# One attention-plus-MLP kernel: loads from three issuing queues instead of one, with a new order of its stages

## The chip, the cores and the metric

The kernel runs on one core of one Trainium2 chip. The metric is the device time of one launch in microseconds: 155.31 us, the median of three runs (155.22 to 155.47).

## What is computed

The inputs are r, k, v, w of shape 4 x 8 x 768 x 48 (batch, heads, sequence, head dimension), u (8 x 48), and the weights of an MLP (384 to 1024 to 384, with a gain vector of 1024), all float32. Two parts follow one another, a recurrence over time and an MLP:

```
for t in range(S):
    cur = einsum("bhd,bhe->bhde", u[None] * k[t], v[t])
    y[t] = einsum("bhd,bhde->bhe", r[t], state + cur)
    state = w[t][..., None] * state + einsum("bhd,bhe->bhde", k[t], v[t])
x = y, laid out as 3072 tokens x 384
h = x @ w_in
solu = h * softmax(h)
out = layernorm(solu) * g_ln @ w_out          # 3072 x 384
```

## The kernel before

The work is cut into 24 units, each of 128 time steps of one batch (six chunks of the sequence times four batches, chunk by chunk). A unit goes through two parts.

Attention: its w, k, r and v are loaded (LW, LK, LR, LV, lines 246 to 256; each 128 partitions x 8 heads x 48 floats, so 1024 pieces of 192 bytes). ScalarE takes the logarithm of w (lw), TensorE cumulates it over time (cum), ScalarE makes the decays of it in PSUM (ex), VectorE multiplies k and r with them (kp), TensorE transposes both (krk, krr) and ScalarE or VectorE copies the result out (kr). TensorE makes the scores (M), which are masked and copied (m; on VectorE with the mask, on ScalarE with a later sel on GpSimd). GpSimd makes the bonus term of u (p, q, in part qh, and dv; VectorE adds up dg). TensorE makes the output of the chunk (Y), which is copied (y), and the new state (S, then et and st).

MLP: x is transposed (X, copied by xT), TensorE makes the hidden layer (H, line 469: 24 matmuls that need all three parts of w_in), ScalarE its exponential (e), VectorE the product (he), ScalarE, VectorE or GpSimd its square (hq), GpSimd in some units the sum of the halves of e (ea), TensorE the output with the column sums for the norm (Oa, Ob, line 496), and small instructions the scale (sq, qm, lv), before ScalarE or VectorE writes the result (o) and it is stored (out, line 536).

The weights come once: w_in in three parts (LI, cast to bfloat16 by wi), w_out in two halves (LO, scaled by gw and centred by ce, with the column mean mn).

The order of everything stands in one string, ORDER (lines 21 to 67). A word is a stage's short name and its unit, and after the point the engine (a ScalarE, d VectorE, p GpSimd) or the PSUM bank. The loop in line 550 emits the stages word by word, and `InOrder` (line 72) makes each engine keep that order: an instruction never overtakes another of the same engine, and a DMA never another of the same queue. All loads and stores are issued by SyncE (SP); an issue waits until its buffer is free. There are seven input buffers of each kind (NIO, line 69), so unit 7 takes the buffers of unit 0. `hot` words are matmuls on zeros in otherwise idle TensorE time.

Of the kernel before, what the change touches and what calls it, by code (L numbers as in the profile page):

```python
# [8 lines left out]
F32 = mybir.dt.float32  # L9
BF16 = mybir.dt.bfloat16  # L10
# [11 lines left out]
LW2 LU0 ik0 lw2 hot5.4 cum2.0 LW1 lw1 us0.7 ih0 LW3 lw3 cum3.2 LR2 uc0 ex2 LK2 p2 LV2 vb2.p kp2 hot4.4 krk2.6 krr2  # L22
LR1 LK1 cum1.4 LW0 ex1 kp1 kr2.d hot1.0 S2.7 lw0 et2 LV1 vb1.d LW4 st2 p1 q1 hot2.0 krk1.1 krr1 q2 qh2 dg2 LG0
kr1.a M2.4 ex3 hot1.0 M1.6 m1.d dv2 LR0 LK0 p0 q0 cum0.0 ex0 lw4 cum4.6 ex4 kp0 krk0.1 krr0 LR3 gs0.0 gc0 dg1
m2.d Y2.i0 kr0.d LK3 p3 LR4 LV0 vb0.a dg0 dv1 kp3 Y1.i5 hot3.1 krk3.4 krr3 LK4 kp4 M0.2 m0.d krk4.1 y1.a X1.5
krr4 y2.a X2.0 dv0 xT2.d hot1.6 Y0.n7 y0.d kr3.a M3.2 hot1.0 X0.6 S1.4 p4 q3 kr4.a xT1.a xT0.a LI2 LI1 wi1.a
M4.0 m4.a et1 LI0 S0.5 et0 wi0.d m3.d LO1 wi2.p H1.6 e1 gw5.a H2.0 e2 H0.2 LO0 gw2.a q4 qh4 dg4 qh3 dg3 gw4.p
gw7.p LV3 vb3.p dv3 sel4 LW6 e0 gw6.d st1 LV4 vb4.p he1 lw6 dv4 gw1.d LW5 gw0.d gw3.d mn0.4 mc0 ce5.p ce6.p
Y3.i7 ce4.p he2 st0 he0 cum6.0 y3.a ce7.p hot1.5 X3.6 lw5 xT3.a ce3.d LK6 LR6 p6 Y4.n5 LR5 LK5 ce2.d hq0.a ex6
LW7 cum5.2 H3.6 p5 y4.d ex5 ce1.d ce0.d Oa0.5 kp6 krk6.1 krr6 S4.0 hq1.d Oa1.4 kp5 krk5.3 krr5 X4.2 Ob1 e3 he3  # L30
LV5 q6 q5 kr5.d hq2.a et4 st4 M5.6 kr6.a M6.0 xT4.d lw7 cum7.2 hq3.a sq1 m6.a m5.d dg5 vb5.d qm1 dv5 Ob0 ex7 sq0
qm0 S3.7 qh6 LR7 LK7 p7 kp7 et3 lv1 st3 lv0 H4.0 Y5.n6 y5.d LR9 LK8 o1.d e4 krk7.3 krr7 Oa2.2 he4 X5.7 q7 kr7.d
LW9 lw9 o0.a LK9 p9 LW8 lw8 S5.6 et5 cum9.4 ex9 Ob2 sq2 LR8 p8 st5 dg6 kp9 qm2 LV6 xT5.a LV9 vb6.p dv6 sel6
cum8.0 ex8 kp8 hq4.a LV7 LV11 out1 LW10 dg7 vb7.p dv7 Oa3.3 vb9.a lv2 H5.6 e5 M7.4 m7.d he5 q8 krk9.1 LK10 krr9
kr9.a S9.0 et9 Ob3 sq3 st9 q9 qm3 o2.a out0 ea5.p Y6.i5 y6.a LV8 LR10 Y7.n4 y7.d LW11 LW12 krk8.1 M9.6 lw10 lv3
X6.2 xT6.a m9.d o3.a krr8 LV10 out3 out2 kr8.d qh9 dg9 dg8 hq5.d cum10.4 ex10 kp10 S6.0 vb11.d et6 X7.2 xT7.a
st6 p10 vb8.d dv8 dv9 H6.6 e6 he6 H7.2 lw11 e7 he7 M8.4 m8.a Oa5.1 Y9.n0 Ob5 sq5 y9.d cum11.6 ex11 krk10.5 krr10
qm5 kr10.d S7.4 et7 st7 Oa4.3 hq6.d lv5 lw12 o5.a X9.2 sel8 Y8.i0 vb10.p y8.a LK11 LR11 kp11 xT9.d q10 dg10 p11
M10.4 m10.a sel10 S10.1 et10 st10 dv10 S8.0 et8 S11.7 et11 X8.6 xT8.a LK12 LW13 cum12.4 q11 ex12 lw13 st11 st8
Ob4 sq4 qm4 LW14 LR12 kp12 p12 lw14 lv4 o4.a out5 LK13 LV12 LR13 Y10.n2 dg11 y10.d H8.6 e8 krk12.1 krk11.0 krr11  # L40
krr12 kr12.d he8 kr11.a q12 qh12 cum13.4 H9.2 vb12.p S12.1 ex13 p13 q13 ea7.p dg12 kp13 dv11 LW16 LR14 LK14 e9
he9 et12 st12 M12.6 m12.a Oa6.0 X10.5 xT10.a krk13.4 krr13 kr13.a M11.6 m11.d ea8.p dv12 sel12 p14 cum14.2 ex14
q14 out4 Ob6 sq6 hq8.d M13.4 m13.d LV13 hq7.a LW15 lw15 lw16 kp14 vb13.d H10.6 dg13 qm6 LW18 lw18 Y11.n1 y11.d
Oa8.5 LK16 LR15 LR16 LK15 e10 he10 hq9.a krk14.4 Y12.i3 krr14 lv6 qh14 kr14.d p15 ea10.p dv13 LR18 LV14 vb14.p
q15 qh15 LK18 p18 Ob8 sq8 qm8 y12.a S13.2 et13 st13 o6.a lv8 X11.1 xT11.d cum16.6 ex16 X12.3 hq10.d LW19 kp16
Oa9.4 cum15.0 xT12.a Ob9 ex15 kp15 sq9 o8.a dg14 dv14 qm9 M14.2 m14.a sel14 krk16.7 Oa7.6 krr16 kr16.d lv9 o9.d
cum18.0 ex18 kp18 Ob7 LV15 S14.5 et14 st14 krk15.3 krr15 kr15.d LK19 Y13.i2 lw19 cum19.0 krk18.7 p16 q16 vb15.a
S15.4 y13.a sq7 qm7 dg15 X13.5 xT13.d ex19 LR19 kp19 lv7 o7.a q18 krr18 kr18.d H11.2 et15 st15 krk19.5 krr19
kr19.d LW17 lw17 cum17.0 e11 he11 ex17 ea11.p out8 LK17 LR17 p17 kp17 H12.6 e12 he12 hq11.a p19 H13.4 e13 Oa10.3
Y14.n2 M16.0 m16.a dg16 q19 dv15 y14.d ea12.p ea13.p M15.6 m15.d he13 Ob10 sq10 X14.2 out9 Oa11.1 LW20 qm10 lw20  # L50
cum20.6 hq12.d krk17.0 krr17 out6 out7 LV16 vb16.a dv16 xT14.a S16.2 LR20 ex20 LK20 dg18 et16 st16 lv10 o10.a
H14.4 e14 kp20 Ob11 sq11 kr17.d LK23 qm11 lv11 o11.a Oa12.2 krk20.3 krr20 kr20.a he14 sel16 Y16.n7 y16.d Y15.n6
y15.d M19.4 m19.a M18.0 m18.d Ob12 X15.7 xT15.a q17 hq13.d LV19 LW21 LV17 X16.3 xT16.a ea14.p vb19.a M17.4 m17.d
sq12 LK22 out10 qm12 dg17 qh19 vb17.p sel19 p20 hq14.a LW22 LV20 q20 qh20 dv17 M20.0 LV21 m20.d out11 LK21 H15.6
e15 he15 lw22 ea15.p H16.4 LV18 vb18.p dv18 LR21 p21 lw21 Oa14.3 Y17.n1 LR22 LV23 q21 dg19 dv19 Ob14 LR23 p23
p22 e16 he16 lv12 Oa13.0 LW23 o12.a out12 sq14 qm14 hq15.d vb20.a lv14 dg20 dv20 y17.d cum21.6 ex21 Ob13 cum22.4
sq13 ex22 LV22 vb22.p ea16.p o14.d out14 Y18.n2 y18.d Oa15.1 X18.3 qm13 kp22 lv13 xT18.d X17.2 xT17.a kp21 Ob15
sq15 qm15 S18.5 et18 st18 Y19.n4 y19.d lv15 o15.a out15 o13.a krk22.2 S17.3 et17 lw23 H18.6 e18 ea18.p hq16.d
vb21.d st17 Y20.n5 y20.d X19.4 xT19.d krr22 kr22.a H17.0 he18 hq18.d cum23.4 ex23 kp23 Oa16.3 e17 ea17.p he17
krk21.2 krr21 kr21.a H19.6 e19 krk23.5 X20.4 krr23 q22 qh21 vb23.p out13 xT20.a kr23.a he19 Oa18.2 Ob16 sq16  # L60
M21.0 q23 ea19.p qh23 dg22 dv22 m21.a sel21 qm16 lv16 M22.6 hq19.a M23.4 Ob18 sq18 dg21 H20.0 o16.a out16 m22.d
m23.d Oa19.7 Y22.n6 qm18 lv18 hq17.d Ob19 S19.5 dg23 dv23 e20 Oa17.4 y22.d X22.3 he20 et19 st19 xT22.d dv21
Y21.n6 Ob17 y21.d sq19 o18.a sq17 qm17 lv17 Y23.n1 out18 qm19 lv19 X21.0 xT21.d H22.2 o17.a e22 out17 ea20.p
y23.d H21.0 X23.5 xT23.a e21 hq20.d o19.d out19 Oa20.6 he22 hq22.d H23.4 e23 he21 hq21.d Ob20 sq20 qm20 lv20
o20.a out20 ea22.p Oa22.7 ea21.p Oa21.3 he23 hq23.d Ob22 sq22 qm22 lv22 Ob21 sq21 qm21 lv21 o21.d o22.a out22
out21 ea23.p Oa23.2 Ob23 sq23 qm23 lv23 o23.a out23
"""

NIO, NLW, NKP, NWK = 7, 10, 6, 4
# [24 lines left out]
def kernel(  # L94
# [26 lines left out]

    nc.scalar.preload_act_table_set("natural_log_exp_and_others")
# [32 lines left out]
    g_rows = consts.tile([KF, 128], F32)  # L155

# [57 lines left out]
    qm_t = ring("qm", NWK, [C, 1], F32)  # L214
    lv_t = ring("lv", NWK, [C, 1], F32)
# [30 lines left out]
    def load_w(i, x):  # L246
        sp.dma_start(out=w_t[i % NIO][:, :, :D], in_=rows_of(w, i))

    def load_k(i, x):
        sp.dma_start(out=kr_t[i % NIO][:, 0, :, :D], in_=rows_of(k, i))  # L250

    def load_r(i, x):
        sp.dma_start(out=kr_t[i % NIO][:, 1, :, :D], in_=rows_of(r, i))

    def load_v(i, x):
        sp.dma_start(out=v_t[i % NIO][:, :, :D], in_=rows_of(v, i))

    def load_u(i, x):
        sp.dma_start(out=u_row, in_=u.rearrange("(o h) d -> o (h d)", o=1))

    def load_g(i, x):
        sp.dma_start(out=g_rows, in_=moe_g_ln.rearrange("(ko ki) -> ko ki", ki=128))

    def load_w_in(j, x):
        sp.dma_start(out=win_f[:, j, :], in_=moe_w_in[j * 128:(j + 1) * 128, :])

    def load_w_out(j, x):
        part = slice(j * KF // 2, (j + 1) * KF // 2)
        sp.dma_start(out=wout_f[:, part, :],
                     in_=moe_w_out.rearrange("(ko ki) d -> ki ko d", ki=128)[:, part, :])  # L270
# [109 lines left out]

    def scores(i, x):
        kr = kr_s[i % NKP]
        m_ps = live[i]["m_ps"] = bank([C, 2, HP, C], F32, x, "m_ps")
        for hp in range(HP):
            for a in range(2):
                rows = slice(64 * a, 64 * a + 64)
                pe.matmul(m_ps[:, a, hp, :], lhsT=kr[rows, hp, :], rhs=kr[rows, HP + hp, :], start=True, stop=True)
# [80 lines left out]

    def hidden(i, x):
        xT = xT_t[i % NWK]  # L470
        h_ps = live[i]["h_ps"] = bank([128, KF, C], F32, x, "h_ps")
# [4 lines left out]

    def hidden_exp(i, x):
        act.activation(out=e_t[i % NWK], in_=live[i]["h_ps"], func=EXP)
# [7 lines left out]
    def hidden_mul(i, x):  # L486
        dve.tensor_mul(out=he_t[i % NWK], in0=live[i]["h_ps"], in1=e_t[i % NWK])

    def hidden_square(i, x):
        he, hq = he_t[i % NWK], hq_t[i % NWK]  # L490
        if x == "a":
            act.activation(out=hq, in_=he, func=SQUARE)
        else:
            (dve if x == "d" else pool).tensor_mul(out=hq, in0=he, in1=he)

    def output(i, part):
        L = live[i]
        e, he, hq, o_ps = e_t[i % NWK], he_t[i % NWK], hq_t[i % NWK], L["o_ps"]
        for f in range(part * KF // 2, (part + 1) * KF // 2):
# [84 lines left out]
```

## Time and profile before

| What | us |
|---|---|
| median of three runs | 155.31 |
| span of the profiled execution, first to last instruction | 152.4 |
| what lies around the span, against the median | 2.9 |
| busy time PE, DVE, ACT, POOL | 136.4, 131.8, 120.0, 119.0 |
| busy time of the warm-up matmuls (tile warm) | 7.8 |
| bytes moved | 27.06 MB |

The profiled execution has no launch time of its own on record, so its span stands for it and the 2.9 us are what the runs have on top. PE is TensorE's matmuls, PEld its weight loads, DVE VectorE, ACT ScalarE, POOL GpSimd, SP SyncE; SPq is SP's queue. Busy time is the union of an engine's instructions, which is a little less than the sum of their durations, since the ends of neighbours overlap. Nearly all instructions carry the line of the helper (L86), so they are told apart by the names of what they read and write.

### The profile page before, as it was taken

What the parts mean: (1) busy time and instruction counts of PE and PEld (TensorE: products, weight loads), DVE (VectorE), ACT (ScalarE), POOL (GpSimd) and SP (SyncE); (2) the same over time, 40 slices, a digit from 0 to 9 for tenths busy, and PEclk for the clock granted to TensorE, in tenths of its full rate; (3) what the DMA queues carried; (4) which work ended last, traced back from release to release, by engine and by line L of the source; (5) the groups of instructions that cost most, each with busy time, mean ns of one, the idle gap of its engine ahead of it and who ended that gap; (6) DMA issues with size and microseconds to landing.
All of it is one profiled execution on the core that took longest, in us unless ns stands there. A gap on an engine that the chain in (4) does not pass through costs nothing.

```text
span 152.4 us, 5172 instructions
## 1 busy us (share of the span) xinstructions
PE 136.4 (90%) x2093; PEld 105.5 (69%) x2093; DVE 131.8 (87%) x227; ACT 120.0 (79%) x247; POOL 119.0 (78%) x149
## 2 busy tenths in 40 slices
PE   6777598968999999999998999999799999999970
PEld 1242365936778889779776689887686988889740
DVE  5029968899999999998999999999999999988940
ACT  4526648869888999799998889998988789938661
POOL 7268986799909994899999997799889979973600
PEclk9959969999999999999999999999999999999998
DMA  3999999989979999989897989995998110112023
GB/s 76 218 216 211 217 334 377 254 175 223 216 151 216 220 204 229 206 177 224 194 203 144 228 195 275 199 199 136 241 205 210 63 45 4 44 63 103 4 79 127
DMA packets 104825, 27.06 MB, mean 178 GB/s; under 512 B 100314, under 2 KB 104419, under 8 KB 104803
## 3 DMA queue, kind: packets, MB, share of 16 engines
q1 hardware_dynamic: 104802, 26.75, 77.4%
q8 instruction: 16, 0.26, 0.7%
q14 instruction: 7, 0.05, 0.1%
HBM read 22.03 MB, written 4.72 MB: 176 GB/s over the span
## 4 chain that ended last, share of the span: by engine, by line
PE 53%; DVE 23%; SPq 8%; ACT 6%; issue 3%; DMA 2%; POOL 1%; DVEq 0%; POOLq 0%
PE ps L86 53%; SPq L86 7%; DVE he L86 6%; DVE m L86 4%; DVE kp L86 4%; DVE w L86 3%; DMA kr_in<-in_k_dram 2%; DVE kr L86 1%; DVE hq L86 1%; DVE y L86 1%; DVE st L86 1%; ACT ps L86 1%; ACT o L86 1%; DVE dg L86 1%; ACT win_sb L86 1%
## 5 line engine op out<-in xcount | busy, mean ns | idle before, releaser
L86 PE MATMUL ps<-w,he 128*128 128x385 bf16 x192 | 44.5, 325 | 1.0 <-DVE w L86 0.7
L86 PE MATMUL ps<-xT,win_sb 128*128 128x128 bf16 x576 | 35.5, 219 | 1.1 <-DVE qm L86 0.8
L86 PEld LDWEIGHTS <-win_sb 128*128 128x128 bf16 x576 | 32.8, 98 | 2.2 <-DVE m L86 0.9
L86 PE MATMUL ps<-one_col,hq 128*128 128x1 bf16 x192 | 31.5, 164 | 0.0
L86 DVE TENSOR_TENSOR he<-ps,e 128x1024 bf16<-128x1024 f32 x24 | 29.1, 1214 | 1.6 <-ACT e L86 1.6
L86 DVE TENSOR_TENSOR kp<-ps,kr_in 128x768 bf16<-128x768 f32 x24 | 22.8, 951 | 7.7 <-DMA kr_in<-in_k_dram 4.9
L86 POOL TENSOR_TENSOR p<-kr_in 128x384 bf16<-128x384 f32 x24 | 24.7, 1038 | 4.5 <-DMA kr_in<-in_k_dram 4.2
L86 POOL TENSOR_TENSOR dv<-vb,dg 128x384 bf16<-128x384 bf16 x24 | 21.7, 907 | 7.5 <-DVE qm L86 3.6
L86 ACT ACTIVATE e<-ps 128x1024 bf16<-128x1024 f32 x24 | 24.5, 1021 | 3.1 <-PE ps L86 2.0
L86 POOL TENSOR_TENSOR ea<-e 128x512 bf16<-128x512 bf16 x17 | 20.0, 1181 | 6.4 <-ACT e L86 5.7
L86 POOL TENSOR_TENSOR q<-p,u_bc 128x384 bf16<-128x384 bf16 x24 | 22.2, 931 | 2.4 <-DVE dg L86 1.7
L86 ACT ACTIVATE ps<-ps 128x768 f32<-128x768 f32 x24 | 19.1, 799 | 5.1 <-PE ps L86 4.3
L86 PEld LDWEIGHTS <-kp 128*128 128x128 bf16 x272 | 17.5, 100 | 6.0 <-DVE kp L86 3.2
L86 PEld LDWEIGHTS <-he 128*128 128x128 bf16 x192 | 18.4, 96 | 4.0
L86 PEld LDWEIGHTS <-hq 128*128 128x128 bf16 x192 | 15.4, 96 | 8.3
L86 DVE TENSOR_TENSOR m<-ps,keep 128x1024 bf16<-128x1024 f32 x15 | 18.2, 1216 | 1.2 <-PE ps L86 1.0
L86 PE MATMUL ps<-ident,kp 128*128 128x128 bf16 x192 | 16.5, 227 | 1.6 <-POOL p L86 1.1
L86 DVE TENSOR_TENSOR hq<-he 128x1024 bf16<-128x1024 bf16 x15 | 13.4, 890 | 0.1
L86 ACT COPY kr<-ps 128x1024 bf16<-128x1024 bf16 x11 | 11.1, 1012 | 2.4 <-PE ps L86 2.4
L86 ACT ACTIVATE lw<-w_in 128x384 bf16<-128x384 f32 x23 | 11.7, 523 | 1.3 <-DMA w_in<-in_w_dram 1.3
L86 PEld LDWEIGHTS <-kr 64*128 64x128 bf16 (+1 forms) x272 | 10.2, 95 | 3.1 <-ACT kr L86 0.7
L86 PE MATMUL ps<-inv_col,ea 128*128 128x1 bf16 x68 | 11.2, 165 | 0.0
(90 smaller groups left out, 293.7 us busy)
## 6 DMA issues: line engine op xcount, KB each, us to landing
w_in<-in_w_dram SPq DMA_DIRECT2D x24, 192.0 KB, 3.7
kr_in<-in_r_dram SPq DMA_DIRECT2D x24, 192.0 KB, 3.7
kr_in<-in_k_dram SPq DMA_DIRECT2D x24, 192.0 KB, 3.7
v_in<-in_v_dram SPq DMA_DIRECT2D x24, 192.0 KB, 3.6
out_dram<-o SPq DMA_DIRECT2D x24, 192.0 KB, 2.6
win_f<-in_moe_w_in_dram SPq DMA_DIRECT2D x3, 512.0 KB, 6.4
wout_f<-in_moe_w_out_dram SPq DMA_DIRECT2D x2, 768.0 KB, 9.0
u_row<-in_u_dram SPq DMA_DIRECT2D x1, 1.5 KB
```

The source lines that it names most:

```text
L86: made = make(*args, **kwargs)
```

## The change

The load functions get an issuing queue from the word: no suffix is SyncE as before, `.a` is ScalarE, `.g` is GpSimd. The instruction then stands in that engine's own order. The same holds for `store`, but all stores stay on SyncE. ScalarE issues 19 loads (6 k, 3 r, 3 w, 5 v, one part of w_in and one half of w_out), GpSimd the v of units 2 to 7 and 14, SyncE the rest.

```
-        sp.dma_start(out=w_t[i % NIO][:, :, :D], in_=rows_of(w, i))
+        queue[x].dma_start(out=w_t[i % NIO][:, :, :D], in_=rows_of(w, i))
...
+    queue = {"": sp, "a": act, "g": pool}
```

The last instruction of `scale` becomes a stage of its own, so that it can be placed apart:

```
     def scale(i, x):
-        act.activation(out=lv_t[i % NWK], in_=sq_t[i % NWK][:, 1:2], func=LN, scale=1e-6 * DF * DF,
-                       bias=qm_t[i % NWK])
+        act.activation(out=lv_t[i % NWK], in_=sq_t[i % NWK][:, 1:2], func=LN,
+                       scale=1e-6 * DF if i in by_rows else 1e-6 * DF * DF, bias=qm_t[i % NWK])
+
+    def root(i, x):
         act.activation(out=rs_t[i % NWK], in_=lv_t[i % NWK], func=EXP, scale=-0.5)
```

Some stages are added that no word of the new order names (transposes by DMA, a hidden layer by rows; `by_rows` is empty), so they emit nothing.

ORDER is written anew as a whole. Its old beginning, up to the stage that stands at 45.09 us of the profile (H4), and its new one, up to the first hidden layer (H1):

```
-LW2 LU0 ik0 lw2 hot5.4 cum2.0 LW1 lw1 us0.7 ih0 LW3 lw3 cum3.2 LR2 uc0 ex2 LK2 p2 LV2 vb2.p kp2 hot4.4 krk2.6 krr2
-LR1 LK1 cum1.4 LW0 ex1 kp1 kr2.d hot1.0 S2.7 lw0 et2 LV1 vb1.d LW4 st2 p1 q1 hot2.0 krk1.1 krr1 q2 qh2 dg2 LG0
-kr1.a M2.4 ex3 hot1.0 M1.6 m1.d dv2 LR0 LK0 p0 q0 cum0.0 ex0 lw4 cum4.6 ex4 kp0 krk0.1 krr0 LR3 gs0.0 gc0 dg1
-m2.d Y2.i0 kr0.d LK3 p3 LR4 LV0 vb0.a dg0 dv1 kp3 Y1.i5 hot3.1 krk3.4 krr3 LK4 kp4 M0.2 m0.d krk4.1 y1.a X1.5
-krr4 y2.a X2.0 dv0 xT2.d hot1.6 Y0.n7 y0.d kr3.a M3.2 hot1.0 X0.6 S1.4 p4 q3 kr4.a xT1.a xT0.a LI2 LI1 wi1.a
-M4.0 m4.a et1 LI0 S0.5 et0 wi0.d m3.d LO1 wi2.p H1.6 e1 gw5.a H2.0 e2 H0.2 LO0 gw2.a q4 qh4 dg4 qh3 dg3 gw4.p
-gw7.p LV3 vb3.p dv3 sel4 LW6 e0 gw6.d st1 LV4 vb4.p he1 lw6 dv4 gw1.d LW5 gw0.d gw3.d mn0.4 mc0 ce5.p ce6.p
-Y3.i7 ce4.p he2 st0 he0 cum6.0 y3.a ce7.p hot1.5 X3.6 lw5 xT3.a ce3.d LK6 LR6 p6 Y4.n5 LR5 LK5 ce2.d hq0.a ex6
-LW7 cum5.2 H3.6 p5 y4.d ex5 ce1.d ce0.d Oa0.5 kp6 krk6.1 krr6 S4.0 hq1.d Oa1.4 kp5 krk5.3 krr5 X4.2 Ob1 e3 he3
-LV5 q6 q5 kr5.d hq2.a et4 st4 M5.6 kr6.a M6.0 xT4.d lw7 cum7.2 hq3.a sq1 m6.a m5.d dg5 vb5.d qm1 dv5 Ob0 ex7 sq0
-qm0 S3.7 qh6 LR7 LK7 p7 kp7 et3 lv1 st3 lv0 H4.0 Y5.n6 y5.d LR9 LK8 o1.d e4 krk7.3 krr7 Oa2.2 he4 X5.7 q7 kr7.d
...
+LW0 LR2.a LW1.a LU0 ik0 LK0.a lw0 hot13.0 cum0.4 us0.1 LW2 LR1 LK1.a lw2 LK2 uc0 LR0 lw1 LW3 LV0.a cum2.2 ex2
+cum1.6 ih0 kp2 ex0 LV2.g hot4.0 krk2.0 krr2 LK3 LR3 LV3.g LW4 ex1 LV4.g LW6 p1 lw3 kp0 kp1 p2 cum3.4 vb0.a p0 S0.1
+LR6 q0 krk0.7 LW7.a krr0 krk1.6 ex3 kr2.d q1 M2.2 vb2.a dg0 kr0.a LK4 kp3 krk3.0 p3 q3 LR4 m2.d lw4 M0.4 m0.d LK6.a
+vb3.a et0 LV1 LW5 krr1 cum4.2 q2 LV5.g kr1.a krr3 dg2 st0 dv0 qh1 vb4.a M1.5 m1.d ex4 p4 S3.7 lw7 Y0.i1 LR5 lw6 dv2
+vb1.p LK5.a LK7.a LR7 LV6.g LG0 LW9 LW8 cum6.4 kp4 ex6 LR9 LV7.g dg1 y0.a lw5 Y2.n6 p6 krk4.2 dg3 LR8 LK8 kr3.d
+S2.3 y2.d dv1 q6 kp6 q4 cum5.0 dv3 LI2.a et2 et3 hot1.6 cum7.4 st3 LR10 LW10 ex5 ex7 S1.6 kp5 st2 krr4 krk6.7 krr6
+kr4.a p5 M3.0 kp7 M4.2 krk5.4 et1 S4.5 LK9 LK10 st1 m3.d LI1 kr6.a X0.0 Y1.i1 dg4 vb6.a lw8 dv4 lw9 vb5.p krr5
+xT0.d X2.7 et4 y1.a Y3.i6 st4 m4.d LO1.a M6.0 y3.a cum8.5 q5 p8 X1.2 LI0 krk7.3 krr7 xT2.a m6.d kr5.a ex8 dg6 xT1.d
+M5.0 gs0.4 kr7.a gc0 dv6 lw10 kp8 m5.d X3.7 S6.2 xT3.d cum9.5 p7 q7 S5.3 Y4.i4 ex9 dg5 wi2.p et6 kp9 et5 vb7.a st6
+LO0 LK11 y4.a cum10.0 ex10 S7.7 kp10 M7.5 krk9.4 Y6.i2 krr9 LV8.a dv5 m7.a krk8.0 krr8 wi1.p st5 qh7 krk10.5 et7
+Y5.i6 gw7.a wi0.p y6.a kr9.d M9.1 p9 gw4.a gw1.p y5.a LW13 LK13 LW11.a gw5.a LW15 kr8.d gw6.a st7 LR13 q9 krr10
+LR11 dg7 m9.d X5.6 H1.3 dv7 LW12 gw3.a gw0.a H3.0 gw2.a e1 e3 mn0.2 LW16 kr10.d sel7 mc0 lw13 ce6.d ce4.d ce0.d
...
```

Over the whole string these engines change (before to after): hq on ScalarE 9 to 18 and on VectorE 15 to 6; kr on ScalarE 11 to 7; xT on ScalarE 15 to 8; m on ScalarE 9 to 8; vb on VectorE 6 to 0, on ScalarE 6 to 9, on GpSimd 12 to 15; gw on ScalarE 2 to 7, on VectorE 4 to 0, on GpSimd 2 to 1; wi from one on each of three engines to three on GpSimd; ce on VectorE 4 to 5, on GpSimd 4 to 3. ea is made for 23 units instead of 17, qh for 8 instead of 12. The warm-up words are 3 with 18 matmuls instead of 9 with 19.

## The prediction

> **What bounds the kernel now.** I read the page's slices first (tenths of busy time in 40 slices of 3.81 us, the last row in GB/s):
>
> ```profile
> PE   6777598968999999999998999999799999999970
> DVE  5029968899999999998999999999999999988940
> DMA  3999999989979999989897989995998110112023
> GB/s 76 218 216 211 217 334 377 254 175 223 216 151 216 220 204 229 206 177 224 194 203 144 228 195 275 199 199 136 241 205 210 63 45 4 44 63 103 4 79 127
> ```
>
> The run has two parts. From slice 11 (42 us) PE is full to the end. Before that it has holes, and DMA is full from slice 1 on, at about 216 GB/s where unit loads move; the 334 and 377 are the MLP weights, whose rows are longer. The stretches say the same (us, busy time of PE, PEld, DVE, ACT, POOL, granted clock, DMA share, GB/s):
>
> ```profile
> 4.00:8.00 4.00, 3.00 (x10) 0.99 (x9) 0.23 (x1) 2.11 (x4) 0.84 (x5) 1.00 1.08 217
> 8.00:12.00 4.00, 3.19 (x22) 1.89 (x22) 1.40 (x2) 1.32 (x3) 2.65 (x4) 0.57 1.09 216
> 24.00:28.00 4.00, 3.58 (x68) 2.77 (x65) 3.34 (x7) 3.05 (x7) 2.18 (x4) 1.00 1.07 372
> 44.00:60.00 16.00, 16.00 (x284) 13.60 (x283) 15.73 (x28) 15.13 (x36) 13.05 (x16) 1.00 0.96 207
> ```
>
> A DMA share over 1 means that the 16 engines have no gap left while 216 GB/s of unit loads move. PE's 3.0 us of 4 in the first row is mostly warm-up. The chain that ended last (start, us, what) shows three things: an early wait for k, and two long runs of PE:
>
> ```profile
> 13.35 3.79 DMA kr_in<-in_k_dram
> ...
> 43.27 31.86 PE ps L86 x551
> ...
> 110.34 37.23 PE ps L86 x601
> ```
>
> Last, SP's queue in order of time. An issue takes 0.4 us while the rings are empty and 0.8 to 1.2 us from the fifth load on, so SP is held back by the engines behind it:
>
> ```profile
> 0.79 0.43 SPq L83 DMA_DIRECT2D w_in<-in_w_dram  x1
> 1.28 0.47 SPq L86 DMA_DIRECT2D u_row<-in_u_dram  x1
> 1.80 1.01 SPq L86 DMA_DIRECT2D w_in<-in_w_dram  x2
> 2.86 1.19 SPq L86 DMA_DIRECT2D kr_in<-in_r_dram  x1
> 4.09 0.85 SPq L86 DMA_DIRECT2D kr_in<-in_k_dram  x1
> ...
> 24.99 4.11 SPq L86 DMA_DIRECT2D v_in<-in_v_dram  x1
> ```
>
> So what decides is how early PE gets enough work to stay full. Its dense work is H and O (the MLP), and H needs w_in.
>
> **The supply, from rows.** kp of unit 2 waits for the fifth load until 7.77; the fifteenth lands at 13.35 + 3.79 = 17.14. That is 0.94 us a load; 196.6 KB at 216 GB/s is 0.91. I use: load n lands at 3.2 + 0.92n. A part of w_in (524 KB at 372 GB/s) adds 1.4 us, a half of w_out 2.1. Check: before has 18 loads ahead of w_in, so 3.2 + 16.6 + 4.2 = 24.0; the last cast of w_in waited for DMA until 25.22 and the first H began at 26.11.
>
> **Step 1, the queues.** The bytes and rows of the loads stay. On three queues the first issues run side by side: SP needed until 2.86 us for its first three loads and u, so at most about 1 us is won in slice 0 (3 tenths of DMA). After that the engines are the limit and a second queue only shares them. By the Trainium skill, "DMA: Bandwidth & Descriptors", section "Issuing engines are not separate DMA queues", loads from several engines run on the same 16 engines and interleave, and only the issue time is saved. The share of 1.08 agrees for one queue; no run yet shows three. By that rule the sum below is what comes.
>
> **Step 2, the order: w_in moves back.** In the new order 41 unit loads (all of units 0 to 7, k, r and w of 8, 9 and 10) stand ahead of LI0, and the cumulations, transposes or products of all of them stand ahead of H1 in PE's order, so PE can't reach H1 without them. Before it was 18. Last part of w_in: 3.2 + 41 x 0.92 + 3 x 1.4 + 2.1 (LO1, on ACT's ring ahead of it) = 47.2; without LO1 45.1. POOL's cast of part 0 takes 1.04 (row wi on POOL: 1037 ns): H1 at 48.3, against 26.1.
>
> Other gates ahead of H1, to see that they hide. DVE: first kp needs the eighth load, 10.6; rows kp 11 x 0.95, m 8 x 1.22, kr 4 x 0.68, st 8 x 0.55, dg 3.9, rest 1.6, together 32.8; DVE's rows overlap (143 summed, 131.8 busy), so 30.2: done at 40.8. ACT: rows 32.6, x 0.9 = 29.3 from its first lw at 3.4, so 32.7, plus 13 DMA issues. POOL: 9 p, 8 q, 2 halves, 7 dv, 2 vb, 2 casts are 27.4 from 10.6, so 38.0, plus three v issues (the first three fall into its wait for data).
>
> **Step 3, what is left after H1.** Before starts H4 at 45.09 and PE ends at 147.57: 102.5 us, nearly gapless. PE's prices here are those from one start to the next in the dense stretch from 44 to 56 us. At H4 it had done, beyond what the new order has done at H1: 4 H (1.34 from start to next start), 2 O (1.7), the column mean (1.4), in all 10.2. The new order has done beyond it 3 cum, 4 krk and krr, 2 M, 2 Y, 3 S (0.33, 0.45, 0.33, 0.38, 0.36 each): 1.0 + 1.8 + 0.7 + 0.8 + 1.1 = 5.4. Left: 102.5 + 4.8 = 107.3. Six more units add halves of e on POOL (ea 17 to 23), which saves 4 small matmuls each at 0.025: 0.6. So 106.7. The tail (sq, qm, lv, rs, o, store) is 152.4 - 147.57 = 4.8 as before; splitting lv into lv and rs moves one 0.20 instruction and adds none.
>
> **Step 4, work between engines.** DVE loses 9 hq (0.89), 6 vb, 4 gw and gains 4 kr, 7 xT: 7 us less. ACT gains 9 hq (1.06) and 5 gw, loses 4 kr, 7 xT: 4 us more. POOL gains 6 ea (1.18), 3 vb, 2 casts, loses 4 halves: 5 more. After H1 that leaves ACT (120.0 busy before, 123.8 with these) 123.8 - 29.3 = 94.5, plus 6 issues at 0.85 = 99.6, under PE's 106.7; DVE 95; POOL about 93. They hide under PE; without that cover ACT would be next. DVE, which held the stretch from 26 to 43 us before, is the engine relieved, but PE's wait for w_in is later than that. Warm-ups are 18 matmuls instead of 19; they lie in idle PE time. In 8 to 12 us the granted clock was 0.57; a longer starved PE may meet more of that, and I take 0, up to 1 us.
>
> **Unknown prices.** No row shows a load issued by ACT or POOL. Both are bounded by SP's issues, 0.39 (nothing queued) to 4.11 (behind the weights). ACT: I take 0.85, SP's usual, so 13 issues are 11 us and it is ready at 43.8, hidden; at 1.7 (two full rings sharing) 54.8, 6.5 us late. What waits behind an issue is ACT's ex, lw and kr copies, and DVE's kp behind those. POOL: nearest is SP's 0.85 too, ready at 40.6, hidden; at 4.11 it is 50.3 and H1 comes 3.2 us later. Below zero nothing is possible but the 1 us of step 1. Loads that leave SP can't wait behind its stores, whose waits for o sum to 22 us, but before 44 us there is no store.
>
> **Sum.** 48.3 + 106.7 + 4.8 = 159.8 span against 152.4. The profiled span lies 2.9 below the median of 155.31; the same on top gives **162.7 us**.
>
> **Rivals.**
> A. *The supply rises, faster.* SP's queue looks solid, and if it was the issuing and not the engines that paced the loads, three queues feed up to three times as fast. The Trainium skill, "Perfetto Trace Analysis", section "DMA Optimizations", says that balancing over the issuing engines may help when the queue looks busy with slices. Then DVE is the gate: first kp at 6.9 (fourth load of SP), 30.2 of work, H1 at about 38, and 38 + 106.7 + 4.8 + 2.9 = 152.4. For: issues solid from 0.8 to 25 us. Against: 0.4 us issues at first, share 1.08, and 372 GB/s from the same queue as soon as rows are longer. It decides where H1 starts before 152.4 - 106.7 - 4.8 = 40.9; with 41 loads that needs 0.79 us a load, 250 GB/s. Chance 0.23.
> B. *No difference.* The rate lands just there, or the shared rate is made up by DVE's relief: 155.3. Chance 0.04.
> C. *The issues are dear.* ACT at 1.7 or POOL at 4 us each come on top: 166 to 169. For: the 4.11 row, and ACT and POOL in the path of every kp and y. Against: both have slack until 47. Chance 0.13.
> The forecast has 0.60, its own range 159 to 165.5 (LO1 behind LI0, a start 1 us earlier; clock and a late ACT above).
>
> So slower by over 0.2% (0.3 us, about what a measurement here can tell from no change) 0.73, within it 0.04, faster 0.23. Range 151.5 to 169: it takes in most of A and of C and leaves out some 0.15.
>
> **What would show it.** Right: GB/s near 216 in slices 1 to 8 and the weights' 330 to 380 about slices 9 to 11; first matmul on win_sb near 48 us; PE tenths with holes until there and 9s after; SP issues over 1 us while ACT also loads. Step 1 is wrong if unit loads move at 250 GB/s or more. Steps 2 and 3 are wrong if H starts near 48 and the end isn't 111 us later. C shows as gaps on ACT or POOL that end with a DMA issue.

## The result, and the profile after

| | us |
|---|---|
| median after, four runs (160.87 to 163.83) | 161.52 |
| median before on the same chip, four runs (153.89 to 155.47) | 155.26 |
| ratio, 95% interval | 1.041 (1.035 to 1.046) |
| span of the profiled execution, after (before 152.4) | 159.1 |
| busy time PE, DVE, ACT, POOL, after | 137.1, 125.6, 123.2, 126.7 |

A run over 1.5% above the fastest of the same kernel counts as slow and is left out of the ratios (one of the four here). The change is slower by 4.1%, some 6.3 us. The forecast was 162.7. Two of its terms were wrong by 2 to 3 us in opposite directions. The slices of the changed kernel give a first view (3.98 us each; last row GB/s):

```profile
PE   6845846898795599999999999997999999999990
DVE  5047991989961999999999999849989999867641
DMA  5999999999999990499998989980182110211122
GB/s 111 258 297 232 257 242 248 294 173 355 381 224 219 205 185 1 126 216 239 229 255 191 196 197 182 234 189 1 54 198 47 59 54 22 81 52 50 56 99 99
```

DMA still is full from slice 1 on, but the unit loads now move at about 250 GB/s instead of 216, with the weights at 355 and 381 in slices 9 and 10. PE's row of holes lasts until slice 13, where before it ended with slice 9; one more dip, in slice 27, is taken up below. The same from the stretches (us, busy time of PE, PEld, DVE, ACT, POOL, granted clock, DMA share, GB/s):

```profile
4.00:8.00 4.00, 3.44 (x15) 1.36 (x14) 0.00 (x0) 2.23 (x5) 3.46 (x8) 1.00 1.27 259
8.00:12.00 4.00, 1.73 (x14) 0.77 (x12) 1.77 (x2) 1.81 (x3) 2.78 (x3) 1.00 1.18 297
24.00:28.00 4.00, 2.59 (x18) 1.56 (x18) 0.64 (x2) 1.03 (x4) 3.98 (x5) 0.57 1.10 248
44.00:60.00 16.00, 12.50 (x188) 10.04 (x187) 11.03 (x16) 11.75 (x21) 12.73 (x15) 1.00 1.02 203
```

A DMA share of 1.08 was taken in the prediction for "no gap left"; here it is 1.27. From 44 to 60 us, where before PE was busy for 16.0 us, it now is for 12.5. The tile of the MLP's weights gives the time of the first hidden layer, in the column of first and last start (26.1 before):

```profile
L86 PE MATMUL ps<-xT,win_sb x576: 216/219/219, 45.6 to 148.1; 128*128 128x128 bf16 x192
```

What stands in front of it are the last cast of w_in on POOL and, on PE, the transpose X of another unit, which waits for its y (start, us, what, and the wait ahead of it):

```profile
43.51 1.04 POOL L86 CAST win_sb<-win_f 128x1024 bf16<-128x1024 f32 x1
45.45 0.34 PE L86 MATMUL ps<-ident,y 128*128 128x128 bf16 x3 [0.18 <-ACT y L86]
```

The cast is through at 44.55, 1.1 us before the first H; the H follows X directly. From there to the end are 159.1 - 45.6 = 113.5 us. The chain that ended last (start, us, what) begins with SP's issues; then it goes through single loads, and two issues of ACT that wait for loads:

```profile
16.53 3.90 DMA kr_in<-in_r_dram
...
21.35 5.41 DMA kr_in<-in_r_dram
26.76 0.02 issue
26.78 0.40 ACTq L86
...
38.31 7.64 DMA kr_in<-in_k_dram
45.96 0.02 issue
45.98 0.39 ACTq L86
```

The issue at 26.78 is that of w_in's part 2, whose buffer nothing had used before. It still waits until an unrelated load of r has landed (21.35 + 5.41 = 26.76): the trace's semaphore events show that the loads of SP and ACT signal their landing on a common set of eight semaphores, and that an issue waits until the load that last had its semaphore is in. On SP such a wait would hold up loads only. On ACT it holds up computing: from 24.3 to 27.3 us ACT computes nothing, and DVE is busy for 0.64 us of the four (third row above).

### The profile page after: what moved, and what is told of

Read it like the earlier page. It is cut to its first block, busy times and chain, and to the rows that moved or that the text cites. A ratio compares the mean times of both kernels' runs of the same rounds, so it can differ in the third digit from the quotient of the medians.

```text
span 159.1 us, 5151 instructions
## 1 busy us (share of the span) xinstructions
PE 137.1 (86%) x2067; PEld 107.4 (68%) x2067; DVE 125.6 (79%) x221; ACT 123.2 (77%) x250; POOL 126.7 (80%) x160
## 3 DMA queue, kind: packets, MB, share of 16 engines
q1 hardware_dynamic: 79170, 20.72, 56.5%
## 4 chain that ended last, share of the span: by engine, by line
PE 37%; DMA 16%; DVE 14%; ACT 13%; SPq 10%; issue 5%; POOL 1%; ACTq 1%; DVEq 0%; POOLq 0%
PE ps L86 37%; SPq L86 10%; DMA kr_in<-in_r_dram 9%; DMA kr_in<-in_k_dram 7%; DVE he L86 4%; ACT e L86 3%; DVE kp L86 2%; ACT o L86 2%; DVE st L86 2%; ACT ps L86 1%; ACT w L86 1%; ACT lw L86 1%; DVE m L86 1%; DVE dg L86 1%; DVE w L86 1%
## 5 line engine op out<-in xcount | busy, mean ns | idle before, releaser
L86 POOL TENSOR_TENSOR ea<-e 128x512 bf16<-128x512 bf16 x23 | 26.9, 1177 | 8.4 <-ACT e L86 7.2
L86 PE MATMUL ps<-one_col,hq 128*128 128x1 bf16 x192 | 31.5, 164 | 0.0
L86 POOL TENSOR_TENSOR p<-kr_in 128x384 bf16<-128x384 f32 x24 | 24.3, 1019 | 3.2 <-DMA kr_in<-in_r_dram 2.4
L86 POOL TENSOR_TENSOR dv<-vb,dg 128x384 bf16<-128x384 bf16 x24 | 19.8, 829 | 7.9 <-DVE dg L86 2.4
L86 ACT ACTIVATE e<-ps 128x1024 bf16<-128x1024 f32 x24 | 24.3, 1019 | 2.0 <-PE ps L86 1.5
L86 ACT ACTIVATE hq<-he 128x1024 bf16<-128x1024 bf16 x18 | 19.0, 1055 | 5.1 <-DVE he L86 5.1
L86 PEld LDWEIGHTS <-kp 128*128 128x128 bf16 x272 | 18.3, 104 | 6.8 <-issue 2.8
L86 PE MATMUL ps<-ident,kp 128*128 128x128 bf16 x192 | 19.0, 237 | 3.0 <-DVE st L86 1.2
L86 DVE TENSOR_TENSOR m<-ps,keep 128x1024 bf16<-128x1024 f32 x16 | 19.4, 1218 | 2.0 <-PE ps L86 1.6
L86 PEld LDWEIGHTS <-hq 128*128 128x128 bf16 x192 | 14.3, 96 | 6.7
L86 PE MATMUL ps<-inv_col,ea 128*128 128x1 bf16 x92 | 15.2, 165 | 0.0
L86 PEld LDWEIGHTS <-kr 64*128 64x128 bf16 (+1 forms) x272 | 11.2, 99 | 5.4 <-issue 1.9
L86 PE MATMUL ps<-lw,uti_neg 128*128 128x384 bf16 x24 | 8.1, 336 | 7.1 <-ACT lw L86 3.4
```

Of the source, the lines that this page charges most:

```text
L86: made = make(*args, **kwargs)
```

## The experiments

All ran beside the kernel before, whose median on their chips lay between 154.31 and 155.36; ratios are against that. Two theories stood after the result. **Theory 1**: the new order is slower because it wants far more loads and attention done ahead of its first dense work, and the queues give back a part of this. **Theory 2**: the issues on ACT and POOL, or some one place in the order, cost the time.

### One queue, two queues, three queues

The new order, with the map of queues changed:

```
e1   queue = {"": sp, "a": sp, "g": sp}
e2   queue = {"": sp, "a": sp, "g": pool}
e3   queue = {"": sp, "a": act, "g": sp}
```

> The new order with every load on SyncE; ScalarE and GpSimd issue none. Theory 1 (the order costs the time: 41 loads and w_in stand ahead of the first H, at the rate that the DMA engines give): the rate falls back from the 257 GB/s seen in the changed kernel at 4 to 8 us to about 216, the first H moves from 45.6 to 48 to 50 us, and the time is 163 to 166 us. Theory 2 (the order is good and the issues on ScalarE and GpSimd cost the time, by stalls such as ScalarE's from 24.3 to 27.3 us): the time falls below 158 us.

> The new order with ScalarE's 19 loads moved to SyncE, GpSimd's seven kept. Theory 1: GpSimd's loads move in packets of about 4 KB and cost the engines less, so the supply is a little over 216 GB/s, first H at 46 to 49 us, 161 to 164 us. Theory 2: ScalarE's stalls at 24 to 27 and 45 to 46 us are gone, and the time is 156 to 159 us.

> The new order with GpSimd's seven loads moved to SyncE, ScalarE's 19 kept. Theory 1: two queues still give about 255 GB/s while both are filled, but SyncE carries seven more loads, so the first H comes at 46 to 49 us and the time is 161 to 164 us. Theory 2 (issues cost): GpSimd gets 7 x 0.93 us back and the time is 160 to 161 us.

| Queues | us | ratio (95%) | first H | GB/s 4 to 8, 8 to 12 us |
|---|---|---|---|---|
| SP (e1) | 167.29 | 1.085 (1.078 to 1.092) | 50.1 | 204, 207 |
| SP, POOL (e2) | 165.07 | 1.070 (1.062 to 1.079) | 48.5 | 213, 281 |
| SP, ACT (e3) | 162.50 | 1.052 (1.045 to 1.060) | 47.3 | 259, 256 |
| all three (the change) | 161.52 | 1.041 (1.035 to 1.046) | 45.6 | 259, 297 |

The kernel before had 154.31 us beside e1 to e3 and 155.26 beside the change, so the ratios are the safer measure across them. The order alone costs 13 us, and the queues give back 5.8 of them by the times and 6.9 by the ratios (0.044 of 155). Against e1, ACT's loads give 4.8 and POOL's 2.2. POOL's share on top of ACT's is 1.0 us by the times and 1.8 by the ratios, whose intervals overlap. No run falls into theory 2's ranges; e1 and e2 lie 1.3 and 1.1 us above theory 1's, e3 within it. The first four microseconds of full supply, SP alone and then SP with ACT:

```profile
4.00:8.00 4.00, 3.68 (x12) 1.34 (x11) 0.00 (x0) 0.72 (x3) 0.63 (x5) 1.00 1.04 204
```

```profile
4.00:8.00 4.00, 3.51 (x13) 1.28 (x12) 0.00 (x0) 1.90 (x5) 0.64 (x5) 1.00 1.28 259
```

The same loads, pieces and engines; a second issuing queue raises the rate by 27%, and the share from 1.04 to 1.28. So the 16 engines had room that one queue did not use. The trace's packet records fit this: a 192-byte piece took 15.5 ns at the mean in e1, and in e3 15.4 on SP's queue and 15.3 on ACT's. Sixteen engines that take one such piece after another move 16 x 192 bytes in 15.5 ns, 198 GB/s, about what one queue gave; the second queue's pieces went beside them and were no slower. By the Trainium skill ("DMA: Bandwidth & Descriptors", section "Issuing engines are not separate DMA queues") a second queue saves issue time only; for these 192-byte pieces the rows say otherwise, and they decide. The Trainium skill's "Perfetto Trace Analysis", section "DMA Optimizations", advises balancing over the issuing engines where generating the descriptors is the bottleneck and not the transfer itself. The 5.8 us agree with the advice; whether its condition held no run shows. POOL's loads help in another way. In the changed kernel (queue, packets, MB, share of 16 engines; q0 is POOL's):

```profile
q1 hardware_dynamic: 79170, 20.72, 56.5%
q0 software_dynamic: 448, 1.38, 2.8%
```

Seven loads in 448 packets are 64 packets a load, where q1's mean is 751 for the same 196.6 KB (its stores and weights, in longer rows, among it). 2.8% of 159.1 us over seven is 0.64 us of the engines a load, against 0.85 at q1's mean (56.5% of 159.1 us for 20.72 MB).

### The old order on three queues

e4 gives the order of before the same 26 suffixes, at the places where its words stand (`LV2` becomes `LV2.g`, `LR2` becomes `LR2.a`, and so on). e7 moves six loads to the very front instead:

```
-LW2 LU0 ik0 lw2 hot5.4
+LW2 LR2.a LK2.a LU0 LK1.a LV2.g LV1.g LV0.g ik0 lw2 hot5.4
```

> The order of before, with the same 26 loads moved to ScalarE and GpSimd and nothing else changed. Theory 1: the queues alone cost nothing or gain a little, 152.5 to 156 us, the first H at 24 to 26 us. Theory 2: the issues on ScalarE wait for landings and hold up its compute, 157 us or more.

> The order of before, with six loads on the other queues at the very front of the order, where no computing stands ahead of them: r and k of unit 2 and k of unit 1 on ScalarE, v of units 2, 1 and 0 on GpSimd; the rest stays on SyncE. Theory 1 (the queues help only at the start, and the order of before is held by the supply for about 1 us, which is what it gained without its unit loads): 153.5 to 155.0, a ratio of 0.990 to 1.000. Theory 2 (any load on a computing engine stops it longer than it brings): 156 or more.

e4 took 188.9 us in its fastest run and 192.4 at the median. Theory 1 is out; theory 2's range is open upwards, but its cause, issues of ACT that wait for a landing, is not what the trace mainly shows. A load on an engine that computes is issued only when the engine gets there, and then its whole way to landing lies in the path. GpSimd in order of time shows it for v of unit 2 (start, us, what, and the wait ahead of it):

```profile
10.74 1.00 POOL L86 TENSOR_TENSOR p<-kr_in 128x384 bf16<-128x384 f32 x1 [5.91 <-DMA kr_in<-in_r_dram]
11.69 1.09 POOL L86 DMA_DIRECT2D v_in<-in_v_dram  x1
16.46 0.49 POOL L86 CAST vb<-v_in 128x384 bf16<-128x384 f32 x1 [3.69 <-DMA v_in<-in_v_dram]
```

The issue needs nothing that p makes, but stands behind it; then POOL waits 3.69 us for what it issued itself. Over the run there are six such waits of POOL, 18.8 us in all, and two of ACT for its own v, 5.8 us. In the kernel before only loads stand ahead of this load. So queue suffixes on the words of an order that was written for one queue do not serve; the places of the loads have to be chosen for them.

e7 took 155.35, ratio 1.006 (1.003 to 1.010): between the two theories, a little slower. The rate rises as it did in e3 (284 GB/s from 4 to 8 us), yet the first product of k and r comes at 8.8 us instead of 7.8: ACT's exponential for it stands behind the logarithm of unit 3's w, and this w, sharing the engines with the six loads, lands only at 7.2.

### What holds up the first hidden layer

e5 moves w_in forward behind 19 unit loads, on SP (three words taken out further back). e12 does that too, moves the casts of w_in about 50 words forward, and puts three hidden layers into banks that are free there:

```
e5  +LR6 LI2 LI1 LI0 q0 krk0.7
e12 +gc0 H1.3 dv6 lw10 e1 kp8 m5.d H2.0 X3.7 S6.2 he1 xT3.d e2 ...
e12 -X5.6 H1.3 dv7 LW12 ... e1 e3 ... he1 ce7.d hq1.a H2.6 ...
```

> The new order with the three loads of w_in moved up, from behind 41 unit loads to behind 19, on SyncE; nothing else is moved, PE's order and POOL's casts neither. Theory 1a (it is the attention of eleven units, which stands ahead of the first H in PE's order, and the unit loads that it needs): the first H stays at 45 to 47 us, the unit loads behind w_in land up to 4 us later, and the time is 161 to 165 us. Theory 1b (it is w_in's late place in the queues alone): the first H comes at 40 us or earlier and the time falls to 156 to 158 us.

> The new order on its three queues with w_in behind 19 loads (as in the run with w_in early, 162.5), and besides the three casts of w_in and the hidden layers of units 1, 2 and 0 with their exponentials and products moved some 60 words towards the front, into banks of PSUM that are free there: the casts behind dv4, vb5 and p8, H1 behind gc0, H2 behind m5, H0 behind kp9 (before, H1 stood behind M9). So fewer units' attention stands ahead of H1. Theory 1 (the place of H1 in TensorE's order is what makes the new order late, since the holes ahead of it have no dense work to fill them): first H at 36 to 39 instead of 47.7, and a time of 157 to 160, against 162.5. Theory 2 (the end is set by what comes behind, the weights of w_out and the outputs, whose places are not moved): first H as early, but a time of 161.5 to 163.

e5: 162.48, ratio 1.051 (1.044 to 1.058), first H at 47.7: theory 1a's time, with H 0.7 us past its range. With w_in issued 22 loads earlier, H1 comes later, not earlier. So the landing of w_in is not what sets it.

e12: 171.64, ratio 1.112 (1.108 to 1.116), against both theories. The first H came at 42.7, not 36 to 39, and 126.9 us were left after it instead of 113. Its chain shows both reasons:

```profile
27.50 2.89 DMA kr_in<-in_r_dram
30.39 0.88 POOL v_in L86
31.28 1.02 POOL p L86
33.03 1.77 POOL q L86 x2
37.29 1.03 POOL win_sb L86
...
42.73 2.75 PE ps L86 x24
45.51 1.03 ACT e L86
46.57 1.23 DVE he L86
...
50.57 1.51 PE ps L86 x24
52.10 1.03 ACT e L86
53.16 1.24 DVE he L86
```

A late r holds up POOL's products, these hold up the casts behind them, and H1 waits for the casts. Then each H is followed by its e on ACT and its he on DVE with little beside them, since DVE's next attention work stands behind he: from 40 to 48 us DVE is busy for 3.10 us and ACT for 3.03, against 6.46 and 5.65 in the changed kernel. (The three casts sit on POOL as in the new order; casts on other engines were not tried.) And as the outputs come later, SP is stopped by a store (its queue's waits from 20 to 85 us: total, times, longest):

```profile
SPq L86 <- ACT sq L86: 17.9, 1, 17.9
```

For 17.9 us no load behind that store is issued. The hidden layers moved alone are worth less than nothing; whether moving the words around them too would mend it was not tried.

### ACT's stop at 24 us

e6 gives ACT's last ten loads to SP (w_in's part 2 and w_out's half among them).

```
-... dv3 LI2.a et2 et3 hot1.6 ... m4.d LO1.a M6.0 ...
+... dv3 LI2 et2 et3 hot1.6 ... m4.d LO1 M6.0 ...
```

> The new order on three queues, with the last ten of ScalarE's 19 loads (one part of w_in, one half of w_out, eight unit loads) moved to SyncE at their places in the order; the first nine stay on ScalarE and the seven on GpSimd. Theory 1 (ScalarE's issues cost little but for their waits for a landing, and what they give is the second queue's rate): ScalarE's stop from 24.3 to 27.3 us goes, and so do the waits of kp for loads that ScalarE issues late (units 20 and 21, 92 to 107 us): 159 to 161 us. Theory 2 (the second queue's rate is worth more than the waits): 162 to 164 us.

162.69, ratio 1.047 (1.039 to 1.055), first H at 45.3: in theory 2's range. The stop goes (ACT and DVE are busy for 6.33 and 6.94 us from 24 to 32, against 5.04 and 4.49), and nothing is won. From 40 to 48 us DVE is busy for 4.73 us instead of 6.46. SP carries ten loads more, and the wait comes later: e6's chain goes through the half of w_out, which takes 9.15 us from its issue at 37.61.

### Without the unit loads

e8 (new order) and e9 (old order) have two input buffers of each kind and load each once; all other unit loads are left out, so the units compute on that data. e10 is e8 with w_in's other parts and the first half of w_out issued by ACT at their places, and k of unit 1 ahead of ACT's first logarithm.

```
+        if ("w", i % NIO) in held:       # likewise for k, r and v
+            return
+        held.add(("w", i % NIO))
-NIO, NLW, NKP, NWK, NHT = 7, 10, 6, 4, 4
+NIO, NLW, NKP, NWK, NHT = 2, 10, 6, 4, 4
e10 -LI1 LI0 LO0
e10 +LI1.a LI0.a LO0.a
```

> The new order on three queues with nearly all unit loads left out: two input buffers of each kind, each loaded once by the first unit that asks for it, so all other units compute on that data (the result is not that of the reference). Weights and stores stay. Theory 1 (the order costs because it asks for 41 loads before the first H): the first H comes at 33 to 38 us, held by VectorE's 30 us of work ahead of it, and the time is 146 to 152 us. Theory 2 (the order itself is bad, apart from the supply): 156 us or more.

> The order of before on SyncE alone with the same loads left out (two buffers of each kind, each loaded once; the result is not that of the reference). Theory 1: the old order asks for 18 loads before the first H and was held by VectorE after it, so it gains less from a free supply than the new order: first H at 20 to 23 us, 147 to 151 us, a gain of 4 to 8 us against 10 to 15 for the new order. Theory 2 (supply is not what tells the orders apart): both gain the same.

> The new order without the unit loads (left out as in the other run without supply: only the first two of each buffer are loaded, so the output is not the reference's), but now the parts of w_in 1 and 0 and the first half of w_out are issued by ScalarE at their places in the order, and k of unit 1 stands ahead of ScalarE's first logarithm, so that the weights don't run ahead of the first k. It asks what the new order gives if no load is ever late at the start. In the other run the first product of k and r began only at 12.4 us, and it took 156.4. Theory 1 (the supply is what keeps the new order behind; break-even of the prediction: first H before 40.9): first product at 8 or before, first H at 37 to 40, time 150.5 to 154. Theory 2 (the order itself is longer, whatever the supply): first H at 40 or later or the rest longer than 113, time 155 or more, against 153.9 of the order of before without its unit loads.

| | us | ratio (95%) | first kp | first H | H to end |
|---|---|---|---|---|---|
| new order, no unit loads (e8) | 156.43 | 1.009 (1.006 to 1.013) | 12.4 | 42.8 | 112.4 |
| old order, no unit loads (e9) | 153.86 | 0.991 (0.988 to 0.995) | 7.7 | 25.9 | 126.1 |
| new order, no unit loads, weights held (e10) | 151.55 | 0.981 (0.977 to 0.986) | 9.6 | 37.7 | 112.6 |

e8's time is in theory 2's range, but it was a flawed test: with few loads to wait for, SP issued three parts of the weights between 2.8 and 5.0 us, among the first loads of k, and the first kp waited until 12.4. e10 mends it, and theory 1 holds but for the first product (9.6 instead of 8 or before): with no load late the first H is at 37.7, and the new order is faster than the old one with or without its loads (153.86, about 155). The old order loses only 1.1 us to its supply (154.97 - 153.86), less than the 4 to 8 that theory 1 of e9 expected, and its first H comes hardly earlier (25.9 against 26.1); the new one loses, by the ratios, 0.059 of 155, some 9 us. (e10 also leaves out most issues on ACT and POOL; e1 to e3 show that these are not the cost.) That even then a part is missing is shown by the stretch behind the first H, in the changed kernel and then in e10:

```profile
48.00:56.00 8.00, 4.68 (x54) 3.23 (x52) 4.74 (x8) 4.77 (x9) 6.39 (x8) 1.00 1.07 210
```

```profile
40.00:48.00 8.00, 5.47 (x54) 4.48 (x52) 5.24 (x8) 4.02 (x6) 7.26 (x9) 0.79 0.00 0
```

The same 54 matmuls and the same hole of PE, once with a full DMA and once with none: this hole is the order's own. PE's wait in it (3.0 us in the changed kernel, 2.5 in e10) ends with DVE's xT5: the next H (`H2.6`) goes into bank 6, which `X5.6` has filled and xT5 must first empty. In DVE's order xT5 stands behind three ce, which wait for the column mean, and ACT copies that behind its gw and two e.

### More loads on POOL

As POOL's loads need less of the engines, e11 gives it k and r of unit 3 as well.

```
-... kp2 ex0 LV2.g hot4.0 krk2.0 krr2 LK3 LR3 LV3.g LW4 ...
+... kp2 ex0 LK3.g LR3.g LV2.g hot4.0 krk2.0 krr2 LV3.g LW4 ...
```

> The new order on its three queues, with k and r of unit 3 issued by GpSimd too, just ahead of its first v (nine loads on GpSimd instead of seven; SyncE's later loads come forward by two). Loads issued by GpSimd take about 0.64 us of the 16 engines instead of 0.91, and seven of them won 2.2 us on top of SyncE alone and 1.0 us on top of SyncE and ScalarE. Theory 1 (up to the first H the new order is held by the supply, as the run without unit loads and with the weights held shows: first H at 37.7 instead of 45.6): two more are worth 0.3 to 1.0 us: first H 44.5 to 45.3, time 160.5 to 161.2, against 161.5. Theory 2 (two more issues of about 0.95 us delay GpSimd's products of r and k, and with them the bonus term and y, by more than they bring): first H at 46 or later, time 162 or more.

165.48, ratio 1.068 (1.062 to 1.073), first H at 48.5: theory 2's time, for another reason than it gave. The rate did rise (309 GB/s from 8 to 12 us, against 297). But the load that was next in need shared the engines with two that were not. In the chain of e11:

```profile
5.92 8.37 DMA w_in<-in_w_dram
14.29 0.02 issue
14.32 0.53 ACT lw L86
```

The w of unit 3 took 8.4 us to land; in the changed kernel its logarithm began at 13.07. The 1.2 us grow along the waits for landings: ACT's issue of w_in's part 2 comes at 28.84 instead of 26.78, and H1 is 2.9 us late.

## Why the prediction was right, point by point

The direction and the size came true, the mechanism only in part: the order costs more than the queues win, as it said, but two of its terms were wrong and cancelled.

- **Step 1, the queues: wrong.** It let the three queues share 216 GB/s and gave them 1 us at the start. The runs show 204 to 207 on SP alone, 256 to 259 with ACT and up to 297 with all three, worth 5.8 us of time (6.9 by the ratios). The share of 1.08, read as "no gap left", was the limit of one queue.
- **Step 2, first H at 48.3: 2.7 us too late, and its gate was wrong.** Measured 45.6. It took w_in's last part for the gate; in e5 this part is issued 22 loads earlier and H1 is 2.1 us later. What held is its other half: the attention of the units ahead must be through before H1 in PE's order. At 256 GB/s, the mean of slices 1 to 6, a load is 0.77 us and 41 of them would be in at 3.2 + 31.5 = 34.7, with the weights' 4.2 + 2.1 at 41.0, and H1 at 42.0; it comes 3.6 us behind that.
- **Rival A's rate came true and its time did not.** It set the limit at 250 GB/s, and the rate passed it. But the 0.79 us a load behind this leave out the 2.1 us of LO1, which the forecast's sum has; with them the limit is 0.74 us, 266 GB/s, and 256 is just short of it. H1 was to be at about 38, by DVE's 30.2 us behind the first kp (6.9 + 30.2 = 37.1, so 38 is rounded up). e10, where no load is late, has 37.7, 28.1 behind its first kp, and 151.55 us (rival A: 152.4). So the price of the order was right, and the step from a mean rate to the landing of each load was not: the loads come from three queues that share the engines, single ones land as late as 5.4 us (the r at 21.35) or 7.6 us (the k at 38.31) behind their issue, 8.4 us in e11, and in-order engines add up the waits. Against e10 the changed kernel's H1 is 45.6 - 37.7 = 7.9 us late.
- **The granted clock, taken as 0 to 1 us: open.** In the changed kernel it was 0.57, 0.50 and 0.65 in the three stretches of 4 us from 24 to 36, where the kernel before and e10 had 1.00. How much of the 7.9 us is this and how much the late loads themselves, no run separates.
- **Step 3, 111.5 from first H to the end: 2.0 too little.** Measured 113.5, and 112.4 to 115.0 in the new order's other runs, e12 apart, whatever their supply. The sum counted PE's work as dense from H1 on; the hole behind it, also in e10, was missed, and so was a stop of PE of about 1.2 us between 104 and 112, behind a load of r that ACT issued at 101.77 and that took 5.13 us to land.
- **Step 4, work between engines: right.** ACT 123.2 busy (123.8 expected), DVE 125.6 (131.8 - 7 = 124.8), POOL 126.7 with its seven issues of about 0.93 (119.0 + 5 expected without them, so some 4 less). But for that one stop they hide under PE after 60 us.
- **Unknown prices.** ACT's issues took 0.37 to 0.54 us, but for two of the first three (0.68 and 1.32; 0.85 was taken), POOL's 0.88 to 1.08. Rival C is refuted by e1 to e3: without these issues it is slower. What the prediction did not name is the wait in front of an issue, for another load's landing or for the engine's own computing. Of these the first cost nothing that e6 could show, and the second, with the waits for what an engine had just issued itself, is what e4's trace shows behind its 189 us.
- **The sum.** 48.3 + 111.5 + 2.9 was forecast; 45.6 + 113.5 + 2.4 came (161.52 - 159.1 = 2.4 around the span; the profiled run itself took 160.87, so 1.8 of it lie around the span and the rest is that it was the fastest of the four). Errors of -2.7, +2.0 and -0.5 leave 1.2 us: that the sum came so close is luck. The direction rests on more than that: H1 would have had to begin by 40.9 (38.9 with the longer rest), and no run of the new order but e10, without its loads, came there.

What stays open: how the new order's 7.9 us of waits could be won back with all loads. None of the full versions beat the kernel before; e7 came nearest.

## What to carry to other kernels

Full DMA engines in the profile of one queue do not mean that the engines are the limit: with small pieces, look at what rate they reach when a second queue issues. But judge an order by when the load next in need lands, and not by the mean rate: in-order engines add up every late landing, and loads sent early on another queue take their rate from it. Put a load on a computing engine only where no work stands ahead of it that waits for something else, since its issue comes no sooner than that work.

## What the runs showed of the hardware

- With 192-byte pieces SP's queue alone moved 204 to 217 GB/s at a DMA share of 1.04 to 1.09; SP's and ACT's together moved 256 to 259 at 1.26 to 1.28. A piece took 15.3 to 15.5 ns either way.
- A load of 196.6 KB issued by GpSimd went in 64 packets, and took 0.64 us of the 16 engines, against 0.85 at the mean of SP's queue. An issue took GpSimd 0.88 to 1.08 us.
- A DMA issue can wait for the landing of a load that has nothing to do with it, and on ScalarE this stopped computing for 3.0 us (24.3 to 27.3).
